# Five loads wait for a matmul: a sigmoid attention with a token-mixing MLP on one core

## The chip, the cores and the metric

The kernel runs on one core of one Trainium2 chip. The time is that of one execution on the device, in microseconds (us). The profile is one further execution, recorded by the hardware profiler; its span runs from the first recorded instruction to the last, and the execution's own time lies a little above its span.

Engines are named as in the profile: PE (TensorE's matmuls), PEld (its weight loads), DVE (VectorE), ACT (ScalarE), POOL (GpSimd), SP (SyncE, which here only issues DMAs).

## The reference

q, k and v have the shape [8, 12, 448, 64] (batch, heads, tokens, width), in float32.

```python
scores = scale * np.matmul(q, k.transpose(0, 1, 3, 2)) - np.log(S)
attn = 1.0 / (1.0 + np.exp(-scores))
x = np.matmul(attn, v)                      # then [8, 448, 768]
wq = x @ w_q                                # [8, 448, 64]
wk = x @ w_k
W_tok = scale * np.einsum('bsd,btd->bst', wq, wk)
mixed = np.einsum('bst,btd->bsd', W_tok, x)
out = np.maximum(mixed, 0.0) @ w_out        # [8, 448, 768]
```

So a sigmoid takes the place of a softmax, and the second half mixes tokens by a matrix that is itself computed from x. Input, output and weights are float32; the matmuls are done in bf16.

## The kernel before, in words

**Tiling.** The work is cut into 24 quads: quad (u, j) is four heads of batch u. A quad has 7 blocks of 64 keys per head. For a block, `scores` (L299) issues four 64x64 matmuls (L303) into a pair of PSUM banks, and ACT takes the sigmoid of the pair into an SBUF tile (L308). `values` (L314) multiplies that tile with v (L321) and gathers the seven blocks of a quad in one pair of banks, which is copied into `xt` (L330). When the three quads of a batch are there, the second half follows for it: transposes of x (L344, L361), the products with w_q and w_k (`mlp_wqk`, L387), a transpose of wk, the product of wk with x (`mlp_tmp`, L431), the mixed tokens with their relu (`mlp_mix`, L471 and L483), and the output product with w_out (L530, L576, L626). The output tiles go to DRAM by stores on SP (L550, L594, L641), some of them held in a list and let go by the letter D of the plan.

**Order.** The order of the instructions on every engine is written out by hand: the string `PLAN` (L127) has a letter for each step (S scores, P and p values, q and k with their variants the bringing of q and k into the layout for the scores, W, N, U, M, O the steps of the second half, D and C stores and copies), and the loop at L840 walks through it. So batch u's second half is interleaved with the attention of later batches.

**Loads.** q, k and v come as one tile of 448 KB for each quad and the six slices of 128 rows of w_out ("w1" to "w6" in the order string, 384 KB each) between them. They are issued in the order of the string `ORDER` (L714), all on SP's queue, by `pump_loads` (L736): each load goes into the next of six fp32 buffers (`lds`, L104), and a load is issued as soon as the tile that was six loads earlier in the same buffer has been cast to bf16. `pump_loads` is called in the program right behind each cast, and so the place of a load in SP's list is settled by the casts. `pump` (L778) issues the casts, on POOL for most tiles, in the order of `ORDER`; a point ahead of a name in `ORDER` puts the cast on DVE (`cast_one`, L787), some steps behind the load. After the casts of q and k of a quad, POOL rearranges the tile (`arrange`, L148) and DVE transposes it (L259, L252).

SP's list holds the loads, the stores and some copies of w_out (L893), and SP works through it in order: a DMA whose semaphore has not come yet holds those behind it.

**Names in the profile.** `ld` is a buffer of a load; `banks` is PSUM; `at` a block of sigmoids; `mx` the mixed tokens; `wkn` and `tmp` are tiles of the second half; `o` is an output tile. The queue q1 carries the loads and stores of SP; q8 carries TensorE's instructions, which are brought from memory in packets while the kernel runs.

Of the kernel before, what the change touches and what calls it, by code (L numbers as in the profile page):

```python
# [17 lines left out]
def kernel(  # L18
# [145 lines left out]

    def load1(n, nm, eng):
        u, j = quads[n]
        if KIND[n] in "cer" and nm != "v":
            t = ld_next()
            eng.dma_start(
                out=t, in_=SRC[nm][u, 4 * j : 4 * j + 4].rearrange("h (p r) d -> (h p) (r d)", r=2 * NI),  # L170
            )
            ld[nm, n] = t
            return
        t = ld_next2()
        eng.dma_start(
            out=t,
            in_=SRC[nm][u, 4 * j : 4 * j + 4].rearrange(
                "(g h) (p i) d -> (h p) g (i d)", g=2, i=NI
            ),
        )  # L180
        ld[nm, n] = t
# [25 lines left out]
    def transposes(ps, t16, r):  # L207

        for x, i in enumerate(range(r.start, r.stop)):
            for g in range(2):  # L210
                for h in range(2):
                    nc.tensor.transpose(  # L212
                        ps[HALF[g], h, x * NP : (x + 1) * NP], t16[HALF[h], i, g, :],
                        ident16[HALF[h], HALF[h]],
                    )

    def transposes_whole(ps, t16, r):

        for x, i in enumerate(range(r.start, r.stop)):
            nc.tensor.transpose(  # L220
                ps[:, x * P : (x + 1) * P], t16[:, i].rearrange("p b d -> p (b d)"), ident16,
            )
# [76 lines left out]
    def scores(n, i):  # L299
        fb, sc, _ = bank2()  # L300
        for g in range(2):
            for h in range(2):
                nc.tensor.matmul(  # L303
                    sc[HALF[h], g, 0:S], qk[n][HALF[g], h, 1, i, :],
                    qk[n][HALF[g], h, 0].rearrange("p i n -> p (i n)"), start=True, stop=True,
                )
        at = p_at.tile([P, 2, S], BF16, tag="at", name="at")
        nc.scalar.activation(at, sc[:, :, 0:S], ACTF.Sigmoid, bias=attn_bias, scale=attn_scale)  # L308
        release(fb)
        ats[n, i] = at  # L310
# [3 lines left out]
    def values(n, i, tail, eng):  # L314
        u, j = quads[n]
        if i == 0:
            pv[n] = bank2()
        fb, ps, _ = pv[n]
        for h in range(2):
            for g in range(2):  # L320
                nc.tensor.matmul(  # L321
                    ps[HALF[g], h, 0:S], ld["v16", n][HALF[h], i, g, :],
                    ats[n, i][HALF[h], g, :], start=(i == 0), stop=(i == NI - 1),
                )
# [10 lines left out]
    def tr_x(n, tail, whole, eng):  # L335
# [3 lines left out]
        if whole:  # L339
            fb, _, ps = bank1()  # L340
            ps = ps.rearrange("p (m g h d) -> p m g h d", m=4, g=2, h=2)
            for h in range(2):
                for m in range(4):
                    nc.tensor.transpose(  # L344
                        ps[:, m, :, h], xt(u, j)[:, h, m * P : (m + 1) * P], ident16
                    )
            for g in range(2) if tail else (slice(0, 2),):
                w = slice((2 * j + g) * P, (2 * j + g + 1) * P) if tail else slice(2 * j * P, 2 * (j + 1) * P)
                COPY["vs"[g] if tail else eng](  # L349
                    out=xns[u][:, :, w],  # L350
                    in_=ps[:, :, g].rearrange("p m h d -> p m (h d)")
                    if tail else ps.rearrange("p m g h d -> p m (g h d)"),
                )
            release(fb)
            return
        fb, _, ps = bank2()
        for m in range(4):
            for h in range(2):
                for g in range(2):
                    for c in range(2):  # L360
                        nc.tensor.transpose(  # L361
                            ps[HALF[c], g, (2 * m + h) * HD : (2 * m + h + 1) * HD],
                            xt(u, j)[HALF[g], h, (2 * m + c) * HD : (2 * m + c + 1) * HD],
                            ident16[HALF[g], HALF[g]],
                        )
# [14 lines left out]
    def mlp_wqk(u, c, tail, act, tiled):  # L380
# [3 lines left out]
        if tiled:  # L384
            for y in range(2):
                for x in range(2):
                    nc.tensor.matmul(  # L387
                        ps[HALF[x], y, 0:S], wqk16[HALF[y], c, 64 * x : 64 * x + 64],
                        xt(u, c // 2)[HALF[y], c % 2, 0:S], start=(c == 0), stop=(c == NC - 1),
                    )  # L390
# [8 lines left out]
        ps = ps[:, 0:S]  # L399
        nc.tensor.matmul(  # L400
            ps, wqk16[:, c, :], xt(u, c // 2)[:, c % 2, 0:S], start=(c == 0), stop=(c == NC - 1),
# [10 lines left out]
    def mlp_wkn(u):  # L412
        fb, _, ps = bank1()
        for m in range(4):
            for c in range(2):
                nc.tensor.transpose(
                    ps[HALF[c], m * DH : (m + 1) * DH],
                    wqks[u % 2][HALF[1], (2 * m + c) * DH : (2 * m + c + 1) * DH],
                    ident16[HALF[1], HALF[1]],
                )  # L420
# [4 lines left out]
    def mlp_tmp(u, act):  # L425
# [3 lines left out]
        for m in range(4):  # L429
            for y in range(2):  # L430
                nc.tensor.matmul(  # L431
                    ps[HALF[y]], wkn[u][:, m, :], xns[u][:, m, y * NB : (y + 1) * NB],
                    start=(m == 0), stop=(m == 3),
                )
# [3 lines left out]
    def mlp_tmp_tiled(u, act):  # L438
# [3 lines left out]
        for m in range(4):  # L442
            for r in range(2):
                if 2 * m + r == NI:
                    continue
                for y in range(2):
                    nc.tensor.matmul(  # L447
                        ps[HALF[y], r, 0:NB], wkn[u][HALF[r], m, :], xns[u][HALF[r], m, y * NB : (y + 1) * NB],
# [12 lines left out]
    def mlp_mix(u, c, act, tail):  # L461
# [5 lines left out]
        if w in TW:  # L467
            for z in range(2):
                for y in range(2):
                    for x in range(2):  # L470
                        nc.tensor.matmul(  # L471
                            ps[HALF[x], y, 256 * z : 256 * z + 256],
# [8 lines left out]
        for y in range(2):  # L481
            for x in range(2):
                nc.tensor.matmul(  # L483
                    ps[HALF[x], y, 0:S], tmps[u][HALF[y], c * P + 64 * x : c * P + 64 * x + 64],
# [33 lines left out]
    def out_pair(act, tail):  # L518
# [8 lines left out]
        for b in range(3 * part, 3 * part + 3):  # L527
            for y, (u, i) in enumerate(blocks):
                for x in range(2):
                    nc.tensor.matmul(  # L530
                        ps[HALF[x], y, 0:NB], mx[HALF[y], u, b, 64 * (i - 3 * y) : 64 * (i - 3 * y) + 64],
# [24 lines left out]
    def out_halves(act, tail):  # L556
# [15 lines left out]
        for c in range(3 * h, 3 * h + 3):  # L572
            t0 = 2 * S * c + m * P + b * NP
            for y in range(2):
                for x in range(2):
                    nc.tensor.matmul(  # L576
                        ps[HALF[x], y, 0:NB], mxs[w][HALF[y], t0 : t0 + NP], wout16[HALF[y], c, x * NB : (x + 1) * NB],
# [28 lines left out]
    def out_chunk(act, tail):  # L606
# [17 lines left out]
        def block(ps, w0, w1, c0, c1):  # L624
            for c in range(c0, c1):
                nc.tensor.matmul(  # L626
                    ps, mxs[w][:, 2 * S * c + m * P : 2 * S * c + (m + 1) * P],
# [48 lines left out]

    def load_wout(c):
        w32[c] = ld_next()[:, 0:D]
        nc.sync.dma_start(out=w32[c], in_=moe_w_out[c * P : (c + 1) * P, :])

# [23 lines left out]
    for _ in range(32):  # L704
        nc.tensor.matmul(pairs[3][:, 0, 0:P], zeros[:, 0:P], zeros[:, 0:P], start=True, stop=True)
    for t in xts:
# [129 lines left out]
    done["q"] = done["k"] = 1  # L836
    nc.tensor.matmul(pairs[free2[0]][:, 0, 0:P], zeros[:, 0:P], zeros[:, 0:P], start=True, stop=True)
    quads_r = []

    for t in PLAN:  # L840
        if t == "F":
            nc.tensor.matmul(pairs[free2[0]][:, 0], zeros[:, 0:P], zeros, start=True, stop=True)
            continue
        if t == "E":
            for g in range(2):
                for h in range(2):
                    nc.tensor.matmul(
                        pairs[free2[0]][HALF[h], g, 0:S], zeros[HALF[g], 0:NP], zeros[HALF[g], 0:S], start=True, stop=True,
                    )
# [94 lines left out]
```

## Time and profile before

| | before |
|---|---|
| time, three runs | 187.07, 186.75, 186.1 us (median 186.75) |
| the profiled execution's own time | 186.47 us |
| its span | 184.7 us |
| granted TensorE clock | 1.00 |
| DMA | 48.51 MB, 263 GB/s in the mean |

How to read it: the shares of busy time are averages over the whole span. The chain of waits follows the work that ended last from the last instruction back to the first, and says for each piece which engine and line, or which wait, it was. "issue" there is time in which an engine waited for nothing that the profile shows. A line `start, us, engine line op` of a timeline is one group of like instructions, with the idle time before it and what ended that in square brackets. A row of busy time by stretch gives the length of the stretch, then busy time and number of instructions for PE, PEld, DVE, ACT and POOL, then the granted clock, the DMA share and GB/s. The DMA rows give, for each queue, packets, MB, and the time of its packets as a share of the 16 DMA engines in that stretch.

### The profile page before, as it was taken

How to read it: one execution, taken by the hardware profiler on the slowest of the kernel's cores; microseconds unless marked ns; L12 is line 12 of the kernel's file. 1: busy time of each engine (PE TensorE's matmuls, PEld its weight loads, DVE VectorE, ACT ScalarE, POOL GpSimd, SP SyncE). 2: the span in 40 equal slices, each digit the busy share in tenths (PEclk: the TensorE clock that was granted, in tenths of full speed). 3: DMA queues.
4: the chain of work that ended last, by engine and by line, in shares of the span. 5: the costliest groups of instructions: out<-in, count | busy, mean ns of one | idle time of the engine just before them, and what ended most of it. 6: DMA issues, size and time to landing. Idle time of an engine off the chain costs nothing.

```text
span 184.7 us, 8546 instructions
## 1 busy us (share of the span) xinstructions
PE 174.6 (95%) x3662; PEld 115.1 (62%) x3662; DVE 133.0 (72%) x209; ACT 162.8 (88%) x209; POOL 124.4 (67%) x171
## 2 busy tenths in 40 slices
PE   7988989999799999999999999999999999999990
PEld 7444645545445464566555778678887878869660
DVE  3424888779598887999797788587668476686820
ACT  4799999999799999999999989999999989876330
POOL 1467799896999599779999996999999920000000
PEclk9999999999999999999999999999999999999999
DMA  5999999969998999988998995897997453422596
GB/s 174 362 383 389 325 382 360 376 209 322 390 331 262 293 350 336 269 304 280 304 281 250 316 330 182 223 362 278 276 307 196 102 136 89 113 65 55 134 240 170
DMA packets 26085, 48.51 MB, mean 263 GB/s; under 512 B 3968, under 2 KB 19968, under 8 KB 26048
## 3 DMA queue, kind: packets, MB, share of 16 engines
q1 hardware_dynamic: 25888, 47.79, 80.0%
q8 instruction: 28, 0.46, 1.0%
q10 hardware_dynamic: 160, 0.20, 0.4%
q14 instruction: 9, 0.07, 0.2%
HBM read 35.78 MB, written 11.01 MB: 253 GB/s over the span
## 4 chain that ended last, share of the span: by engine, by line
PE 73%; ACT 17%; issue 3%; DVE 2%; DMA 2%; ACTq 0%; POOL 0%; SPq 0%
PE banks L303 16%; ACT at L308 16%; PE banks L530 15%; PE banks L321 13%; PE banks L626 12%; PE banks L387 3%; PE banks L576 3%; PE banks L431 2%; DMA ld<-in_k_dram 2%; PE banks L344 2%; PE banks L361 2%; PE banks L471 2%; PE banks L212 1%; PE banks L447 1%; PE banks L483 1%
## 5 line engine op out<-in xcount | busy, mean ns | idle before, releaser
L308 ACT ACTIVATE at<-banks 128x896 bf16<-128x896 f32 x168 | 141.4, 931 | 5.5 <-PE banks L303 4.8
L303 PE MATMUL banks<-qk 64*64 64x448 bf16 x672 | 62.0, 358 | 2.1 <-ACT at L308 1.4
L321 PE MATMUL banks<-at,v 64*64 64x448 bf16 x672 | 45.7, 351 | 0.4 <-ACT at L308 0.4
L303 PEld LDWEIGHTS <-qk 64*64 64x64 bf16 x672 | 25.8, 105 | 22.6 <-issue 13.6
L188 POOL CAST qk<-ld 128x896 bf16<-128x896 f32 x28 | 33.1, 1194 | 7.3 <-issue 1.9
L530 PE MATMUL banks<-wout,mx 64*64 64x384 bf16 x672 | 36.9, 323 | 0.1
L321 PEld LDWEIGHTS <-v 64*64 64x64 bf16 x672 | 22.8, 106 | 9.4 <-issue 2.7
L330 DVE CAST xt<-banks 128x896 bf16<-128x896 f32 x19 | 20.7, 1089 | 10.6 <-PE banks L321 10.1
L530 PEld LDWEIGHTS <-mx 64*64 64x64 bf16 x672 | 23.5, 106 | 4.3 <-issue 0.8
L626 PE MATMUL banks<-wout,mx 128*128 128x384 bf16 (+1 forms) x138 | 24.9, 320 | 0.0
L459 DVE TENSOR_SCALAR mx<-banks 128x1024 bf16<-128x1024 f32 (+2 forms) x21 | 21.1, 1011 | 3.9 <-PE banks L471 1.8
L198 POOL CAST v<-ld 128x896 bf16<-128x896 f32 x23 | 21.6, 955 | 2.0 <-DMA ld<-in_v_dram 1.8
L626 PEld LDWEIGHTS <-mx 128*128 128x128 bf16 x138 | 12.0, 98 | 10.3 <-issue 4.6
L157 POOL COPY swap<-qk 32x448 uint32<-32x448 uint32 x28 | 16.3, 583 | 1.7
L259 DVE STREAM_TRANSPOSE qk<-qk 128x448 f32<-128x448 f32 x28 | 17.4, 630 | 0.0
L163 POOL COPY qk<-swap 32x448 uint32<-32x448 uint32 x28 | 16.1, 577 | 1.6
L160 POOL COPY qk<-qk 32x448 uint32<-32x448 uint32 x28 | 16.1, 576 | 1.6
L539 DVE COPY o<-banks 128x768 f32<-128x768 f32 x11 | 10.5, 953 | 6.2 <-PE banks L530 4.6
L374 DVE COPY xn<-banks 128x1024 bf16<-128x1024 bf16 (+1 forms) x14 | 9.0, 649 | 3.2 <-PE banks L361 2.7
L198 POOL CAST q<-ld 128x896 bf16<-128x896 f32 x7 | 7.0, 999 | 1.8 <-DMA ld<-in_q_dram 1.4
L387 PE MATMUL banks<-xt,wqk 64*64 64x448 bf16 x120 | 8.0, 349 | 0.0
L349 DVE COPY xn<-banks 128x1024 bf16<-128x1024 bf16 x9 | 6.1, 683 | 1.3 <-PE banks L344 1.1
(94 smaller groups left out, 203.8 us busy)
## 6 DMA issues: line engine op xcount, KB each, us to landing
ld<-in_q_dram SPq DMA_DIRECT2D x24, 448.0 KB, 5.7
ld<-in_v_dram SPq DMA_DIRECT2D x24, 448.0 KB, 5.6
ld<-in_k_dram SPq DMA_DIRECT2D x23, 448.0 KB, 6.0
out_dram<-o SPq DMA_DIRECT2D x42, 192.0 KB, 4.9
ld<-in_moe_w_out_dram SPq DMA_DIRECT2D x6, 384.0 KB, 6.3
out_dram<-ld SPq DMA_DIRECT2D x11, 192.0 KB, 2.8
wout<-wout SPq DMA_DIRECT2D x12, 96.0 KB, 5.5
out_dram<-ld SPq DMA_DIRECT2D x4, 96.0 KB, 2.3
```

Of the source, the lines that this page charges most:

```text
L157: eng.tensor_copy(out=z[lo], in_=w[hi, 0])
L160: eng.tensor_copy(out=w[hi, 0], in_=w[lo, 1])
L188: COPY[e](out=f[:, :, "qk".index(nm)].rearrange("p e i d y -> p e y i d"), in_=ld.pop((nm, n)).rearrange("p (y i e d) -> p e y i d", y=2, ...
L198: COPY[e](out=t16.rearrange("p i b d -> p b i d"), in_=ld.pop((nm, n)).rearrange("p b (i d) -> p b i d", i=NI),)
L259: nc.vector.transpose(out=qk[n][:, t].rearrange("p t i n -> p (t i n)").bitcast(F32), in_=w)
L303: nc.tensor.matmul(sc[HALF[h], g, 0:S], qk[n][HALF[g], h, 1, i, :], qk[n][HALF[g], h, 0].rearrange("p i n -> p (i n)"), start=True, stop=True,
L308: nc.scalar.activation(at, sc[:, :, 0:S], ACTF.Sigmoid, bias=attn_bias, scale=attn_scale)
L321: nc.tensor.matmul(ps[HALF[g], h, 0:S], ld["v16", n][HALF[h], i, g, :], ats[n, i][HALF[h], g, :], start=(i == 0), stop=(i == NI - 1),)
L330: COPY[eng](out=xt(u, j)[:, :, 0:S], in_=ps[:, :, 0:S])
L459: nc.vector.tensor_scalar(dst, ps, moe_scale, 0.0, ALU.mult, ALU.max)
L530: nc.tensor.matmul(ps[HALF[x], y, 0:NB], mx[HALF[y], u, b, 64 * (i - 3 * y) : 64 * (i - 3 * y) + 64], wout16[HALF[y], slot(y, b), x * NB : ...
L626: nc.tensor.matmul(ps, mxs[w][:, 2 * S * c + m * P : 2 * S * c + (m + 1) * P], wout16[:, c, w0:w1], start=(c == 0), stop=(c == NC - 1),)
```

## The change

All matmuls and transposes on TensorE are now issued through `mm` and `mt`, which also keep them in a list, `products`, in order of issue. A table `BEHIND` names five loads and for each the number of a product. `pump_loads` issues such a load only once that product stands in the list, and gives it a semaphore wait on that product's end. `pump_loads` and `pump` are also called at the head of each step of the plan, so that a load that was held back in the program is issued when its product is there. Nothing is computed otherwise, and no tile or buffer changes.

The five loads are slice w1 (rows 0 to 127) of w_out, v of quads 8, 20 and 23, and q of quad 22.

```diff
+    products = []
+
+    def mm(*args, **kw):
+        products.append(nc.tensor.matmul(*args, **kw))
+
+    def mt(*args, **kw):
+        products.append(nc.tensor.transpose(*args, **kw))
...
+    def behind_product(load, m):
+
+        if m > 0:
+            tc.add_manual_dep(
+                load.ins, products[m].ins.name,
+                mybir.DependencyInfo(mybir.DependencyClass.Sync, mybir.DependencyReason.DATA),
+                reason="loads begin behind a matmul",
+            )
...
-    def load_wout(c):
+    def load_wout(c, m):
         w32[c] = ld_next()[:, 0:D]
-        nc.sync.dma_start(out=w32[c], in_=moe_w_out[c * P : (c + 1) * P, :])
+        behind_product(nc.sync.dma_start(out=w32[c], in_=moe_w_out[c * P : (c + 1) * P, :]), m)
...
+    BEHIND = {("w", 1): 728, ("v", 8): 856, ("q", 22): 2264, ("v", 20): 2392, ("v", 23): 2648}
...
             nm, n = ORDER[len(loaded)]
+            m = BEHIND.get((nm, n), 0)
+            if m >= len(products):
+                break
             if len(ring) >= 6 and ring[-6] not in cast:
                 break
             ring.append((nm, n))
             if nm == "w":
-                load_wout(n - 1) if n else load_weights()
+                load_wout(n - 1, m) if n else load_weights()
             else:
-                load1(n, nm, nc.sync)
+                load1(n, nm, nc.sync, m)
...
     for t in PLAN:
+        pump_loads()
+        pump()
         if t == "F":
```

`load1` passes its DMA through `behind_product` in the same way, and every `nc.tensor.matmul` and `nc.tensor.transpose` of the kernel becomes `mm` or `mt`.

More of the change, by code (lines that the diff above doesn't have):

```diff
@@ L168, in load1 @@
             t = ld_next()
-            eng.dma_start(
-                out=t, in_=SRC[nm][u, 4 * j : 4 * j + 4].rearrange("h (p r) d -> (h p) (r d)", r=2 * NI),
+            behind_product(
+                eng.dma_start(
+                    out=t, in_=SRC[nm][u, 4 * j : 4 * j + 4].rearrange("h (p r) d -> (h p) (r d)", r=2 * NI),
+                ), m,
             )
@@ L174, in load1 @@
         t = ld_next2()
[L175 to L179, printed above, removed]
+        behind_product(
+            eng.dma_start(
+                out=t,
+                in_=SRC[nm][u, 4 * j : 4 * j + 4].rearrange(
+                    "(g h) (p i) d -> (h p) g (i d)", g=2, i=NI
+                ),
+            ), m,
         )
@@ L211, in transposes @@
                 for h in range(2):
-                    nc.tensor.transpose(
+                    mt(
                         ps[HALF[g], h, x * NP : (x + 1) * NP], t16[HALF[h], i, g, :],
@@ L302, in scores @@
             for h in range(2):
-                nc.tensor.matmul(
+                mm(
                     sc[HALF[h], g, 0:S], qk[n][HALF[g], h, 1, i, :],
@@ L320, in values @@
             for g in range(2):
-                nc.tensor.matmul(
+                mm(
                     ps[HALF[g], h, 0:S], ld["v16", n][HALF[h], i, g, :],
@@ L343, in tr_x @@
                 for m in range(4):
-                    nc.tensor.transpose(
+                    mt(
                         ps[:, m, :, h], xt(u, j)[:, h, m * P : (m + 1) * P], ident16
@@ L360, in tr_x @@
                     for c in range(2):
-                        nc.tensor.transpose(
+                        mt(
                             ps[HALF[c], g, (2 * m + h) * HD : (2 * m + h + 1) * HD],
@@ L386, in mlp_wqk @@
                 for x in range(2):
-                    nc.tensor.matmul(
+                    mm(
                         ps[HALF[x], y, 0:S], wqk16[HALF[y], c, 64 * x : 64 * x + 64],
@@ L399, in mlp_wqk @@
         ps = ps[:, 0:S]
-        nc.tensor.matmul(
+        mm(
             ps, wqk16[:, c, :], xt(u, c // 2)[:, c % 2, 0:S], start=(c == 0), stop=(c == NC - 1),
@@ L415, in mlp_wkn @@
             for c in range(2):
-                nc.tensor.transpose(
+                mt(
                     ps[HALF[c], m * DH : (m + 1) * DH],
@@ L430, in mlp_tmp @@
             for y in range(2):
-                nc.tensor.matmul(
+                mm(
                     ps[HALF[y]], wkn[u][:, m, :], xns[u][:, m, y * NB : (y + 1) * NB],
@@ L446, in mlp_tmp_tiled @@
                 for y in range(2):
-                    nc.tensor.matmul(
+                    mm(
                         ps[HALF[y], r, 0:NB], wkn[u][HALF[r], m, :], xns[u][HALF[r], m, y * NB : (y + 1) * NB],
@@ L470, in mlp_mix @@
                     for x in range(2):
-                        nc.tensor.matmul(
+                        mm(
                             ps[HALF[x], y, 256 * z : 256 * z + 256],
@@ L482, in mlp_mix @@
             for x in range(2):
-                nc.tensor.matmul(
+                mm(
                     ps[HALF[x], y, 0:S], tmps[u][HALF[y], c * P + 64 * x : c * P + 64 * x + 64],
@@ L529, in out_pair @@
                 for x in range(2):
-                    nc.tensor.matmul(
+                    mm(
                         ps[HALF[x], y, 0:NB], mx[HALF[y], u, b, 64 * (i - 3 * y) : 64 * (i - 3 * y) + 64],
@@ L575, in out_halves @@
                 for x in range(2):
-                    nc.tensor.matmul(
+                    mm(
                         ps[HALF[x], y, 0:NB], mxs[w][HALF[y], t0 : t0 + NP], wout16[HALF[y], c, x * NB : (x + 1) * NB],
@@ L625, in block @@
             for c in range(c0, c1):
-                nc.tensor.matmul(
+                mm(
                     ps, mxs[w][:, 2 * S * c + m * P : 2 * S * c + (m + 1) * P],
@@ L704 @@
     for _ in range(32):
-        nc.tensor.matmul(pairs[3][:, 0, 0:P], zeros[:, 0:P], zeros[:, 0:P], start=True, stop=True)
+        mm(pairs[3][:, 0, 0:P], zeros[:, 0:P], zeros[:, 0:P], start=True, stop=True)
     for t in xts:
@@ L836 @@
     done["q"] = done["k"] = 1
-    nc.tensor.matmul(pairs[free2[0]][:, 0, 0:P], zeros[:, 0:P], zeros[:, 0:P], start=True, stop=True)
+    mm(pairs[free2[0]][:, 0, 0:P], zeros[:, 0:P], zeros[:, 0:P], start=True, stop=True)
     quads_r = []
     for t in PLAN:
+        pump_loads()
+        pump()
         if t == "F":
-            nc.tensor.matmul(pairs[free2[0]][:, 0], zeros[:, 0:P], zeros, start=True, stop=True)
+            mm(pairs[free2[0]][:, 0], zeros[:, 0:P], zeros, start=True, stop=True)
             continue
@@ L846 @@
                 for h in range(2):
-                    nc.tensor.matmul(
+                    mm(
                         pairs[free2[0]][HALF[h], g, 0:S], zeros[HALF[g], 0:NP], zeros[HALF[g], 0:S], start=True, stop=True,
```

4 lines of the change are left out of this document (2 added, 2 removed).

## The prediction

> **What bounds the kernel now.** I read the busy shares first, then the queues of the page, then busy time by stretch.
>
> ```profile
> PE 174.6 (95%) x3662; PEld 115.1 (62%) x3662; DVE 133.0 (72%) x209; ACT 162.8 (88%) x209; POOL 124.4 (67%) x171
> ...
> q8 instruction: 28, 0.46, 1.0%
> ```
> ```profile
> 52.00:160.70 108.70, 108.63 (x2410) 74.48 (x2406) 85.90 (x119) 104.74 (x129) 86.46 (x119) 1.00 0.81 257
> ```
>
> TensorE is the bound: from 52.0 to 160.7 us PE is busy 108.63 of 108.70 at the full granted clock. A load can gain nothing there by coming earlier. Time is to be had only where PE stands. The chain of waits around 49 us shows the largest such place, and the timelines of the weight loads and of ACT what it does.
>
> ```profile
> 49.34 0.75 issue
> 50.09 0.32 PE banks L431
> ```
> ```profile
> 48.50 0.47 PEld L431 LDWEIGHTS <-wkn 128*64 128x64 bf16 x8 [0.20 <-issue]
> 50.34 0.11 PEld L303 LDWEIGHTS <-qk 64*64 64x64 bf16 x4 [1.38 <-issue]
> ```
> ```profile
> 50.84 2.54 ACT L308 ACTIVATE at<-banks 128x896 bf16<-128x896 f32 x3 [0.99 <-PE banks L303]
> ```
>
> PE stands 0.75 us for nothing that the profile names ("issue"), ahead of the last matmul of a group at L431 whose operands are all there. The weight loads pause 1.38 us (48.97 to 50.34), and ACT, the second busiest engine, then starves for 0.99 us. What is missing is the instructions themselves. Their queue, q8, brought 28 packets for the 3662 + 3662 instructions: 7324/28 = 262 to a packet, some 128 products with their weight loads. The counts of products fit that:
>
> ```profile
> 0.00:50.05 50.05, 44.88 (x863) 25.74 (x864) 32.69 (x63) 46.09 (x57) 36.15 (x51) 1.00 0.96 333
> 50.05:131.33 81.28, 80.87 (x1664) 50.99 (x1664) 68.24 (x95) 78.75 (x98) 71.68 (x97) 1.00 0.89 291
> ```
> ```profile
> 131.35 0.27 PEld L530 LDWEIGHTS <-mx 64*64 64x64 bf16 x8 [0.45 <-issue]
> ```
>
> The stall stands ahead of product 863 (counted from 0). A second, shorter pause stands 1664 = 13 x 128 products later, ahead of 2527. So packet borders lie at 735 + 128k. The DMA view by stretch shows the packet that the first stall waits for, and that of the second:
>
> ```profile
> q1 hardware_dynamic: 550, 1.29, 98.3%
> ```
> ```profile
> q8 instruction: 1, 0.02, 6.2%
> ```
> ```profile
> q1 hardware_dynamic: 416, 0.88, 76.2%
> ```
> ```profile
> q8 instruction: 1, 0.02, 6.1%
> ```
>
> These are 43.9 to 47.67, 47.67 to 48.7, 125.7 to 128.9 and 128.9 to 130.0 us. In the first, loads move and no instructions do; in the second (of which, and of the fourth, the row of q8 is shown) the packet passes in 0.062 x 16 x 1.03 = 1.02 us, and TensorE goes on 1.39 us after its end (48.70 to 50.09). In the third pair likewise: nothing, then a packet until some 130.07, and work again 1.3 us later, at 131.35.
>
> I read the request as made when TensorE enters the packet before, that is at border 735 (44.0 us, below) for the packet from 863. It then waited 3.7 us. What was ahead of it is in SP's timeline and the issue-to-landing times:
>
> ```profile
> 41.12 0.38 SPq L175 DMA_DIRECT2D ld<-in_v_dram  x1
> 41.75 0.34 SPq L679 DMA_DIRECT2D ld<-in_moe_w_out_dram  x1
> 42.63 0.34 SPq L169 DMA_DIRECT2D ld<-in_q_dram  x1
> 43.41 1.56 SPq L679 DMA_DIRECT2D ld<-in_moe_w_out_dram  x2
> 47.98 0.38 SPq L175 DMA_DIRECT2D ld<-in_v_dram  x1
> ```
> ```profile
> ld<-in_v_dram SPq DMA_DIRECT2D x1, 448.0 KB, 5.1
> ```
> ```profile
> ld<-in_q_dram SPq DMA_DIRECT2D x1, 448.0 KB, 7.2
> ```
>
> v7 (issued 41.12) lands at 46.2, q10 (42.63) at 49.8. The packet, 47.67 to 48.70, passed behind v7 and the weight rows "w1" and in the midst of q10, but ahead of the next weight rows (43.41), issued 0.6 us before the request.
>
> **The change part by part.** Five loads get one wait each on the end of a product: 728, 856, 2264, 2392, 2648, each 7 products ahead of a border (735, 863, 2271, 2399, 2655). In the instruction order PE, DVE, ACT and POOL keep every place; PE gets five semaphore updates on matmuls that exist. On SP, w1, v8 and v20 keep their places; q22 and v23 move behind the two stores each that followed them; q14's load and two stores swap. When those products ran, by their counts:
>
> ```profile
> 0.00:43.30 43.30, 39.08 (x729) 22.39 (x730) 27.58 (x57) 39.54 (x50) 31.64 (x45) 1.00 0.95 330
> 0.00:48.51 48.51, 44.05 (x857) 25.38 (x858) 31.69 (x63) 44.74 (x56) 34.96 (x49) 1.00 0.95 332
> 0.00:120.88 120.88, 115.34 (x2266) 68.86 (x2270) 92.22 (x146) 114.63 (x142) 98.12 (x134) 1.00 0.92 307
> 0.00:125.67 125.67, 120.13 (x2393) 72.42 (x2396) 96.11 (x152) 119.19 (x148) 102.55 (x140) 1.00 0.92 309
> ```
> ```profile
> 118.01 0.33 SPq L169 DMA_DIRECT2D ld<-in_q_dram  x1
> 118.43 4.72 SPq L550 DMA_DIRECT2D out_dram<-o  x6
> 125.37 0.39 SPq L175 DMA_DIRECT2D ld<-in_v_dram  x1
> ...
> 135.18 0.37 SPq L175 DMA_DIRECT2D ld<-in_v_dram  x1
> ```
>
> Each product starts at the end of its row and takes some 0.36 us, so the loads can go at about 43.7, 48.9, 121.2 and 126.0.
>
> *w1*: 41.75 becomes 43.7, 2.0 us later; behind it on SP wait q10 (+1.5 at most) and the two weight loads from 43.41 (+1.2 to +0.4). Nothing held is then ahead of the request of 44.0 but v7: the load of 43.41 went 0.6 before it and came behind, and w1 now goes 0.3 before it. The packet starts when v7 is through, by 46.2, passes until 47.2 and is usable 1.4 later, at 48.6. The weight load that needs it is due at 48.97. Margin 0.3 to 0.4: the stall goes, with little to spare. Its worth is at least PE's 0.75 and at most ACT's 0.99, since ACT has sigmoids queued and the next scores wait for it; I take 0.9, nearer to ACT's.
>
> *v8*: 47.98 becomes 48.9, with q11 and k11 behind it +0.5. There is no stall at 991, so this gains nothing by itself; it keeps v8 from standing ahead of the request at 863, which comes 0.9 earlier once the first stall is gone.
>
> *q22, v20*: these hold the next gain. q22 goes 2 to 3 us later and its place is taken by stores of L550; v20 goes at most 0.7 later, or none when TensorE is 0.9 ahead. The packets for 2399 and 2527 come earlier by what no longer stands in front. At 2527 the weight loads' pause is 0.45, against 0.20 at a plain join (the row of 48.50): 0.2 taken, between 0 and 0.45. If these two packets did not come earlier, the 0.9 would be lost again there: TensorE 0.9 ahead would meet them where they are.
>
> ```profile
> q1 hardware_dynamic: 243, 0.33, 99.9%
> q8 instruction: 1, 0.02, 6.2%
> ```
>
> That is 123.5 to 124.4: the packet for 2399, at the end of which 1.3 us lead to 125.7, just when 2399 is reached. It has no slack already.
>
> *v23*: issued 0.5 to 1.5 later, no stall near it; nothing.
>
> *Cover of the later landings.* Who takes the delayed data:
>
> ```profile
> 49.92 1.19 POOL L188 CAST qk<-ld 128x896 bf16<-128x896 f32 x1 [0.35 <-DMA ld<-in_q_dram]
> ```
> ```profile
> 63.51 1.19 POOL L188 CAST qk<-ld 128x896 bf16<-128x896 f32 x1 [1.92 <-issue]
> ```
> ```profile
> 63.75 0.62 DVE L259 STREAM_TRANSPOSE qk<-qk 128x448 f32<-128x448 f32 x1
> ```
> ```profile
> 56.98 1.13 DVE L198 CAST v<-ld 128x896 bf16<-128x896 f32 x1
> ```
> ```profile
> 133.96 1.20 POOL L188 CAST qk<-ld 128x896 bf16<-128x896 f32 x1
> 135.08 0.93 POOL L198 CAST v<-ld 128x896 bf16<-128x896 f32 x1
> ...
> 147.59 0.93 POOL L198 CAST v<-ld 128x896 bf16<-128x896 f32 x1
> ```
>
> q10's cast already waits for its landing, so POOL's row of casts and rearrangements comes up to 1.5 late. It ends at 61.59, 1.92 ahead of POOL's next cast and 2.2 ahead of the transposition of its result: hidden. v8, landed by 53.0, is cast on DVE at 56.98; q22 (landing near 127) at 133.96; v20 (near 129) at 135.08; v23 (140) at 147.59. All hidden by 4 us and more, and no buffer's return moves, since each is freed by its cast.
>
> **Sum**: 0.9 + 0.2 = 1.1 us. The profiled execution took 186.47 (184.7 of span and 1.77 around it), so 185.37 against its own time. The median of the runs shown is 186.75, and the mean of the four times 186.6. From these 185.5 to 185.65 follow: **185.6**.
>
> **The rivals.**
>
> *No effect on the packet.* If the request is made otherwise than I read it, or w1's descriptors at 43.7 still get ahead of it, the packet stands behind w1 as before. A half of the stall, or all, stays: 186.2 to 186.8. For it: the margin is 0.3. Against it: the load of 43.41 came behind.
>
> By the Trainium skill, "DMA: Bandwidth & Descriptors", section "Queues, rings and completion order", each DMA engine takes turns between its queues, packet by packet. By that rule a request would pass after one packet of the loads, and holding loads would be worth nothing: 186.6. The trace speaks against it: the 3.8 us without a q8 packet above.
>
> *The wall.* The first stall goes, and the packets for 2399 or 2527 come no earlier, since six stores and k- and v-loads fill the engines in q22's place. Then 0.7 to 0.9 is lost again there: 186.3 to 186.7. For it: the 99.9% share around 124.0. Against it: 448 KB less stand in front of the packet.
>
> *Slower.* SP takes its list in order, so w1's wait holds q10 and two weight loads, and the engines run empty for a moment. If q10's landing comes more than 1.9 later than 49.8, POOL's chain eats its pause at 63.5 and its next casts run late; from 2.2 DVE's transposition is late too and with it the scores. At 4 us, with the instructions' packet and w1 ahead of q10, TensorE would wait about 2 us, against 1.1 won: 187.6. Against it: q10 is issued only 1.5 later, behind the same bytes.
>
> **How the numbers follow.** Forecast 0.58 (185.1 to 186.0), no effect 0.18 (0.06 of it for the turns between queues), wall 0.14, slower 0.10. What this kernel's measurement can tell from no change is 0.5%, 0.93 us, so the border is 185.82, close to the forecast; 0.05 of the forecast's chance lies above it. Faster 0.53, same 0.37, slower 0.10. The range 185.0 to 186.9 leaves out the slower rival and the forecast's edge. Both ends of the unknown costs lie in it: 0.75 + 0 gives 185.85, 0.99 + 0.45 gives 185.16 from 186.6.
>
> **What would show it.** Right: the "issue" of 0.75 us in the chain before product 863 is gone, ACT's 0.99 at 50.84 too, and the q8 packet passes by 47.3; PE's weight loads show no pause above 0.25 at 2399 and 2527. Wrong: the packet still passes after 47.6; or a new "issue" of some 0.9 at a border in 120 to 132 us; or POOL's idle time "<-DMA" grows by over 2 us between 48 and 64 and PE waits for DVE or POOL behind it.

## The result, and the profile after

The changed kernel takes 185.54 us (median of 8 runs, 185.22 to 186.15), the kernel before 187.13 us (8 runs, 186.1 to 189.43). The ratio is 0.9926, with a 95% interval of 0.9902 to 0.9950: 0.5 to 1.0% faster. A ratio is that of the means (here 185.62 and 187.00 us); an execution over 1.5% above the fastest of its kernel, as the one of 189.43 us, counts as slow and is left out of it. The profiled execution of the changed kernel took 185.81 us, with a span of 184.0.

The busy shares of the page say that the work is the same; the busy time of PE is 174.7 us for 174.6:

```profile
PE 174.7 (95%) x3662; PEld 115.3 (63%) x3662; DVE 133.1 (72%) x209; ACT 162.7 (88%) x209; POOL 124.3 (68%) x171
```

What has changed is where TensorE stands. Every matmul is now issued from one helper, so the rows have its lines (L119, transposes L122), and groups are told apart by tiles. First the weight loads and ACT around product 863, in the changed kernel (start, us, engine, line, operation, tile, count, idle time before it):

```profile
48.98 0.47 PEld L119 LDWEIGHTS <-wkn 128*64 128x64 bf16 x8 [0.20 <-issue]
49.75 0.11 PEld L119 LDWEIGHTS <-qk 64*64 64x64 bf16 x4 [0.30 <-issue]
```
```profile
47.77 5.82 ACT L329 ACTIVATE at<-banks 128x896 bf16<-128x896 f32 x7
```

The pause of 1.38 us in the weight loads is 0.30, which is what this join costs without a stall (the same 0.30 stands at this join where no packet border is near it, in experiment 6). ACT's idle 0.99 us is gone: seven sigmoids stand in a row. Next SP, and the DMA queues from 44.4 to 45.8 and from 45.8 to 46.8 us:

```profile
44.22 0.34 SPq L700 DMA_DIRECT2D ld<-in_moe_w_out_dram  x1
44.65 0.38 SPq L187 DMA_DIRECT2D ld<-in_q_dram  x1
45.13 0.86 SPq L700 DMA_DIRECT2D ld<-in_moe_w_out_dram  x2
```
```profile
q1 hardware_dynamic: 254, 0.48, 96.4%
```
```profile
q1 hardware_dynamic: 145, 0.35, 98.5%
q8 instruction: 1, 0.02, 6.1%
```

w1 goes at 44.22, and the packet of instructions that passed at 47.68 to 48.70 before passes at 45.8 to 46.8 now. The border at 735 is reached at 44.45, so it waited 1.4 us and not 3.7. The DMA engines are no less busy (96 to 98%): the packet does not pass because the engines are free; what differs is that w1 was ordered 2.0 us later against the border.

The second pause, ahead of 2527, is gone too. At 2399 one is left, in the changed kernel's weight loads:

```profile
125.54 0.46 PEld L119 LDWEIGHTS <-mx 64*64 64x64 bf16 x12 [0.34 <-issue]
```
```profile
130.26 0.56 PEld L119 LDWEIGHTS <-mx 64*64 64x64 bf16 x12
```

In before these two rows had 0.17 and 0.45.

**Where the time went, by stretches.** The starts of TensorE's weight loads, by their number, divide an execution well, since all 3662 are in each trace. The long stretches between the borders repeat to 0.01 us in all these kernels (991 to 2271: 63.35 or 63.36; 864 to 991: 7.18 or 7.19, but for one; 2784 to 3552: 27.56 or 27.57), so that nearly the whole difference can be read off a few columns. "Wait" is from the weight load of 735, where I take the request to be made, to the start of the packet for 863. All are us of the one profiled execution. That the request is made at a border is inferred: in each of these traces exactly one packet starts between two borders of 735 + 128k, the earliest 0.06 us behind its border. Experiment 6 has other numbers and stands apart.

| kernel | wait | 862 to 864 | 864 to 991 | 2398 to 2400 | 2526 to 2528 | 223 to 3661 |
|---|---|---|---|---|---|---|
| before | 3.70 | 1.49 | 7.19 | 0.29 | 0.56 | 164.73 |
| changed | 1.37 | 0.42 | 7.19 | 0.46 | 0.10 | 163.57 |
| 1 w1 alone | 2.23 | 0.42 | 7.18 | 0.67 | 0.56 | 164.08 |
| 2 all but w1 | 2.78 | 0.48 | 7.18 | 0.15 | 0.10 | 163.40 |
| 3 order, no wait | 3.01 | 0.76 | 7.19 | 0.14 | 0.10 | 163.67 |
| 4 all 64 earlier | 3.29 | 1.05 | 7.19 | 1.56 | 0.10 | 165.36 |
| 5 w1 at 776 | 1.59 | 0.42 | 8.61 | 0.15 | 0.10 | 164.78 |
| 7 q22 at 2296 | 2.05 | 0.42 | 7.19 | 0.14 | 0.10 | 163.31 |
| 8 w1, q22, v20 | 1.54 | 0.42 | 7.19 | 0.15 | 0.10 | 163.34 |
| 9 changed again | 1.26 | 0.42 | 7.19 | 0.15 | 0.10 | 163.31 |
| 10 w1, q22 | 2.57 | 0.42 | 7.19 | 0.14 | 0.69 | 163.71 |
| 11 w1 at 715 | 2.97 | 0.72 | 7.19 | 0.14 | 0.10 | 163.61 |
| 12 v19 for q22 | 2.46 | 0.42 | 7.18 | 0.14 | 0.09 | 163.73 |

0.42, 0.14 and 0.10 are the joins without a pause. After an undelayed join at 2527, 0.23 us are given back in the two stretches behind it (2528 to 2784 takes 10.95 for 10.72), so the 0.56 there cost 0.23. Before to changed: 1.07 won at 863, 0.17 lost at 2399, 0.23 won at 2527, in all 1.16 from 223 to the end (0.03 is left to other places). The starts differ too: product 223 begins at 15.33 in before and 15.81 in the changed kernel, and anywhere from 15.33 to 16.43 in the kernels of the table. Up to there the changed kernel issues its loads in the same order as before and none of them is held, so this is not the change. With this later start the two profiled executions as a whole lie only 0.66 us apart (186.47 and 185.81).

### The profile page after: what moved, and what is told of

The parts are those of the page before. It is cut to its first block, busy times and chain, and to the rows that moved or that the text cites. A ratio compares the mean times of both kernels' runs of the same rounds, so it can differ in the third digit from the quotient of the medians.

```text
span 184.0 us, 8547 instructions
## 1 busy us (share of the span) xinstructions
PE 174.7 (95%) x3662; PEld 115.3 (63%) x3662; DVE 133.1 (72%) x209; ACT 162.7 (88%) x209; POOL 124.3 (68%) x171
## 4 chain that ended last, share of the span: by engine, by line
PE 78%; ACT 14%; issue 3%; DVE 2%; ACTq 0%
PE banks L119 73%; ACT at L329 13%; PE banks L122 6%; DVE xt L351 1%; DVE mx L480 1%; ACTq L661 0%; DVE ld L680 0%; DVE wqk L426 0%; ACT xt L349 0%; ACT wq L428 0%; ACT ld L678 0%; DVE zeros L716 0%; ACTq L329 0%; ACTq L678 0%; ACTq L428 0%
## 5 line engine op out<-in xcount | busy, mean ns | idle before, releaser
L119 PE MATMUL banks<-wout,mx 64*64 64x384 bf16 (+2 forms) x954 | 68.5, 323 | 0.0
L119 PE MATMUL banks<-qk 64*64 64x448 bf16 x672 | 61.8, 358 | 2.0 <-ACT at L329 1.3
L119 PEld LDWEIGHTS <-mx 64*64 64x64 bf16 (+1 forms) x954 | 41.1, 105 | 14.4 <-issue 5.1
L119 PE MATMUL banks<-at,v 64*64 64x448 bf16 x672 | 45.6, 351 | 0.2
L119 PEld LDWEIGHTS <-qk 64*64 64x64 bf16 x672 | 25.5, 105 | 21.4 <-issue 12.6
L209 POOL CAST qk<-ld 128x896 bf16<-128x896 f32 x28 | 33.6, 1210 | 5.4 <-DVE qk L280 1.4
L119 PEld LDWEIGHTS <-v 64*64 64x64 bf16 x672 | 22.7, 106 | 9.2 <-issue 2.4
L165 POOL COPY swap<-qk 32x448 uint32<-32x448 uint32 x28 | 15.7, 562 | 1.7
L122 PEld LDWEIGHTS <-xt 64*64 64x64 bf16 (+1 forms) x528 | 10.9, 107 | 3.6 <-issue 2.4
L119 PE MATMUL banks<-xt,wqk 64*64 64x448 bf16 (+1 forms) x138 | 12.7, 350 | 0.1
L122 PE MATMUL banks<-ident,xt 64*64 64x64 bf16 (+1 forms) x528 | 12.4, 198 | 0.1
L119 PE MATMUL banks<-wqk,tmp 64*64 64x256 bf16 (+1 forms) x72 | 8.9, 298 | 0.1
L119 PE MATMUL banks<-wq,tmp 64*64 64x256 bf16 (+1 forms) x72 | 9.0, 300 | 0.0
```

The costliest lines, as they stand in the source:

```text
L119: products.append(nc.tensor.matmul(*args, **kw))
L122: products.append(nc.tensor.transpose(*args, **kw))
L165: eng.tensor_copy(out=z[lo], in_=w[hi, 0])
L209: COPY[e](out=f[:, :, "qk".index(nm)].rearrange("p e i d y -> p e y i d"), in_=ld.pop((nm, n)).rearrange("p (y i e d) -> p e y i d", y=2, ...
```

## The experiments

Theory: a packet of TensorE's instructions, requested one packet ahead, waits in the DMA engines for the loads that were issued before the request; the holds let loads go so late that the packet gets ahead of them (w1 goes 0.23 us before the request wherever it is held at 728). Rivals: the order on SP does it (C), the waits themselves (D), the later loads alone (B), the first gain needs no second one (A).

**1. w1 alone.**

```diff
-    BEHIND = {("w", 1): 728, ("v", 8): 856, ("q", 22): 2264, ("v", 20): 2392, ("v", 23): 2648}
+    BEHIND = {("w", 1): 728}
```

> Only the weight rows w1 wait (for product 728); v8, q22, v20 and v23 are issued as before. Theory (TensorE's instruction packets stand in the DMA engines behind loads that were issued earlier): the stall ahead of product 863 is gone, TensorE is some 0.9 us ahead behind it, and loses most of that again at the borders 2399 and 2527, whose packets come no earlier: ratio to before 0.996 to 1.000. Rival A (the later packets come earlier by themselves when TensorE is ahead): the 0.9 stays, ratio 0.9945 to 0.996. Rival B (what q22, v20 and v23 do is all of the gain): the stall ahead of 863 stays, ratio 1.000.

Measured: 186.17 us, ratio 0.9946 (0.9921 to 0.9972). The profiled execution, 186.46, does what the theory says: 863 is free, and its weight loads stop at 2399 and 2527:

```profile
125.95 0.46 PEld L119 LDWEIGHTS <-mx 64*64 64x64 bf16 x12 [0.56 <-issue]
```
```profile
131.33 0.27 PEld L119 LDWEIGHTS <-mx 64*64 64x64 bf16 x8 [0.45 <-issue]
```

Against 163.31 without a pause it has 164.08: 0.53 lost at 2399 and 0.23 at 2527. This is the wall. The ratio lies with rival A, though. The twelve times fall in two groups, three from 185.12 to 185.25 and nine from 186.07 to 186.46, and the profile is of the upper one; it fits that the wall is met in most executions and missed in some, but no trace of a lower one was taken. By its time this kernel can't be told from the changed kernel.

**2. All but w1.**

```diff
-    BEHIND = {("w", 1): 728, ("v", 8): 856, ("q", 22): 2264, ("v", 20): 2392, ("v", 23): 2648}
+    BEHIND = {("v", 8): 856, ("q", 22): 2264, ("v", 20): 2392, ("v", 23): 2648}
```

> The other four loads wait, w1 does not. Theory: the packet for product 863 again stands behind w1, the stall of about 0.75 us ahead of 863 stays; at 2399 and 2527 up to 0.4 us is saved: ratio to before 0.997 to 1.000. Rival B (the gain is that of the late loads): ratio 0.992 to 0.994.

Measured: 186.29 us, ratio 0.9967 (0.9935 to 0.9998), as the theory has it. Its interval just touches what rival B gave (0.992 to 0.994); what rules rival B out is experiment 1, where 863 is free with w1 alone held and the interval leaves out 1.000. In the trace the late pauses are gone, but the pause at 863 is short this time:

```profile
50.24 0.11 PEld L119 LDWEIGHTS <-qk 64*64 64x64 bf16 x4 [0.37 <-issue]
```

The stretch from 862 to 864 is 0.06 over the plain join, where 0.75 was expected: a miss in size. w1 was issued later here (42.98, 1.9 us ahead of the request at 44.87, for 2.2 in before), and the packet waited 2.78 and not 3.70.

**3. The order alone.**

```diff
-        if m > 0:
+        if m < 0:
             tc.add_manual_dep(
```

> The order of all lists is that of the changed kernel (q22 and v23 behind two stores each), but no load has the wait on a product. Theory: w1 goes at about 41.8 us as before, the packet for 863 stands behind it, the stall stays: ratio to before 0.997 to 1.001. Rival C (the order on SP, not the waits, makes the gain): ratio 0.992 to 0.994 and no stall ahead of 863.

Measured: 186.71 us, ratio 0.9990 (0.9960 to 1.0020). The gain needs the waits; rival C falls. The trace has the pause at 863 (0.76 - 0.42 = 0.34 us over the plain join) and none at 2399 and 2527: q22 behind two stores was enough there in this execution.

```profile
50.73 0.11 PEld L119 LDWEIGHTS <-qk 64*64 64x64 bf16 x4 [0.65 <-issue]
```

**4. The same waits, 64 products earlier.**

```diff
-    BEHIND = {("w", 1): 728, ("v", 8): 856, ("q", 22): 2264, ("v", 20): 2392, ("v", 23): 2648}
+    BEHIND = {("w", 1): 664, ("v", 8): 792, ("q", 22): 2200, ("v", 20): 2328, ("v", 23): 2584}
```

> The same five loads wait for products, each 64 products earlier (664, 792, 2200, 2328, 2584). The waits and the five semaphore updates are there, but w1's is over before its buffer is free. Theory: w1 goes as before, ahead of the request for the packet: the stall ahead of 863 stays, ratio 0.997 to 1.001. Rival D (the waits or updates themselves change TensorE's flow, or any later load helps): ratio 0.992 to 0.994.

Measured: 186.89 us, ratio 0.9999 (0.9966 to 1.0032). Rival D falls: five waits and five updates that come half a packet earlier are worth nothing. The pauses are back, at 863 and, larger than in before, at 2399:

```profile
50.30 0.11 PEld L119 LDWEIGHTS <-qk 64*64 64x64 bf16 x4 [0.94 <-issue]
```
```profile
127.23 0.46 PEld L119 LDWEIGHTS <-mx 64*64 64x64 bf16 x12 [1.45 <-issue]
```

**5. w1 later still.**

```diff
-    BEHIND = {("w", 1): 728, ...
+    BEHIND = {("w", 1): 776, ...
```

> As the changed kernel, but w1 waits for product 776 instead of 728: it and the loads behind it on SP (q10 and two weight loads) go some 2.4 us later still, at about 46.6 us, with the packet for 863 long ahead of them. Theory with the prediction's arithmetic: q10 lands 2.4 to 2.9 us later than before's 49.9, POOL's chain of casts takes up its pause of 1.9 us, DVE's transposition (2.2 to 3.4 us of slack) is late by at most 0.7: ratio to before 0.992 to 0.996, and TensorE waits for nothing but at most 0.5 us on DVE or POOL. Rival (waiting loads cost at once what they are late): TensorE waits some 2 us between 50 and 70, ratio 1.000 to 1.004.

Measured: 187.37 us, ratio 1.0033 (0.9996 to 1.0069). This is the rival's side. No border has a pause, and 1.42 us are lost between 864 and 991. SP's list, the waits of PE, the chain of waits and PE's timeline say for what:

```profile
47.29 0.34 SPq L700 DMA_DIRECT2D ld<-in_moe_w_out_dram  x1
47.73 0.38 SPq L187 DMA_DIRECT2D ld<-in_q_dram  x1
48.20 0.86 SPq L700 DMA_DIRECT2D ld<-in_moe_w_out_dram  x2
```

```profile
PE banks L119 <- DVE wout L790: 1.4, 1, 1.4
```
```profile
48.67 6.65 DMA ld<-in_moe_w_out_dram
...
55.42 0.57 DVE wout L790
```
```profile
54.33 0.34 PE L119 MATMUL banks<-wout,mx 128*128 128x384 bf16 x1
56.03 0.48 PE L119 MATMUL banks<-wout,mx 128*128 128x384 bf16 x2 [1.37 <-DVE wout L790]
```

It is not q10 and POOL, but the second of the two weight loads behind them on SP: it lands at 55.33, is cast on DVE by 55.99, and the output product that needs it stood 1.37 us. In the changed kernel the same two casts run together at 52.14:

```profile
52.14 1.40 DVE L790 CAST wout<-ld 128x768 bf16<-128x768 f32 x2
```

There the same load, issued at 45.60, landed at 52.36. In experiment 5 the cast ended 0.66 us behind the landing, and the output product was due at 56.03 - 1.37 = 54.66, so that landing was due at 54.00. The changed kernel is 0.19 earlier there (864 begins at 49.75 and not 49.94), so its landing is due at 53.81: the cover of the hold at 728 is 1.4 to 1.5 us. That agrees with the loss: against TensorE, w1 went 3.07 - 0.19 = 2.88 us later in experiment 5 than in the changed kernel, and 1.42 of it was lost. By this estimate a hold that came 1.5 us later would begin to cost.

**6. Other numbers, same kernel before.**

```diff
-    for _ in range(32):
-        nc.tensor.matmul(pairs[3][:, 0, 0:P], zeros[:, 0:P], zeros[:, 0:P], start=True, stop=True)
+    for _ in range(64):
+        nc.tensor.matmul(pairs[3][:, 0, 0:64], zeros[:, 0:P], zeros[:, 0:64], start=True, stop=True)
```

> The kernel before, with 64 warm-up matmuls of 64 columns in place of 32 of 128 (their results are not used): every later product has a number 32 higher, and nothing else moves. Theory (packets of TensorE's instructions hold 128 products, borders at 735 + 128k by number): packets pass and pauses stand at the same numbers as before, 863 and the like, which are now other matmuls, 32 earlier in the plan; the matmul that stalled before (now number 895) runs without a pause. The time depends on which loads stand in front there: ratio 0.990 to 1.004. Rival (the pause belongs to that matmul, its operands or its time): it stays ahead of the same matmul, now number 895, at about 49 to 50 us.

Measured: 187.89 us, ratio 1.0035 (0.9997 to 1.0073). The join that stalled in before runs plainly, and the pauses have gone to other matmuls:

```profile
50.82 0.11 PEld L303 LDWEIGHTS <-qk 64*64 64x64 bf16 x4 [0.30 <-issue]
```
```profile
42.81 0.28 PEld L344 LDWEIGHTS <-xt 128*128 128x128 bf16 x5 [1.00 <-issue]
```
```profile
63.00 0.11 PEld L321 LDWEIGHTS <-v 64*64 64x64 bf16 x2 [1.34 <-issue]
```

These stand at the numbers 735 and 1119, which is 863 - 128 and 863 + 2 x 128. Where a pause can stand is a matter of a matmul's number, not of its operands. Which loads stood ahead of these two packets was not followed here.

**7. q22 later.**

```diff
-    BEHIND = {... ("q", 22): 2264 ...
+    BEHIND = {... ("q", 22): 2296 ...
```

> As the changed kernel, but q22 waits for product 2296 instead of 2264, and so goes about 1.2 us behind the request for the packet of 2399 instead of 0.4. In the changed kernel's trace that packet took 2.02 us to pass (122.16 to 124.18) with q22's data beside it, against some 1.0 us for most, and TensorE paused 0.3 us ahead of 2399. Theory (a load issued just behind the request still shares the engine with the packet): the packet passes in about 1.0 us, the pause goes: 0.1 to 0.3 us less than the changed kernel, ratio to before 0.990 to 0.9925. Rival (the 2.02 us comes from the stores in front): the packet still takes 2 us, ratio as the changed kernel, 0.9926, or up to 0.994 if the stores behind q22 come late.

Measured: 186.61 us, ratio 0.9982 (0.9945 to 1.0020): not the 0.990 to 0.9925 that the theory expected, and beyond the rival's 0.994. Yet the profiled execution, 185.75, shows what the theory expected: the packet passes in 0.88 us, and 163.31 is the time without any pause. Its packets for 2527 to 3039 came within 0.1 to 0.3 us of being late, by the 1.3 us that they need behind their end; in other executions they may have been late. But experiment 10's packets for 2911 and 3039 came as narrowly, and its ratio is 0.9934. Why this kernel gains so little was not traced and stays open.

**8. w1, q22 and v20.**

```diff
-    BEHIND = {("w", 1): 728, ("v", 8): 856, ("q", 22): 2264, ("v", 20): 2392, ("v", 23): 2648}
+    BEHIND = {("w", 1): 728, ("q", 22): 2264, ("v", 20): 2392}
```

> Only w1, q22 and v20 wait; v8 and v23 are issued as before. Theory: those three do all of the work, the stalls at 863, 2399 and 2527 are gone, ratio to before 0.992 to 0.994. Rival (v8 must wait too, since it stands ahead of the packet for 863 or 991; or v23, for 2655 or 2783): a pause of 0.3 us or more at one of these borders, ratio 0.995 to 0.998.

Measured: 185.86 us, ratio 0.9959 (0.9921 to 0.9996); the profiled execution took 185.4. The ratio is on the rival's side, the trace on the theory's: no pause at any border, 163.34. The weight loads at 2399 and 2527 join plainly, with no idle time named:

```profile
125.11 0.48 PEld L119 LDWEIGHTS <-mx 64*64 64x64 bf16 x12
```
```profile
129.88 0.56 PEld L119 LDWEIGHTS <-mx 64*64 64x64 bf16 x12
```

Whether v8 and v23 are worth anything in other executions is not told apart, since the interval holds the changed kernel's ratio.

**9. The changed kernel again**, with nothing altered, beside 10 to 12.

> The changed kernel itself, beside the three others on the same chip. Expected: ratio to before 0.990 to 0.995, as in the result; no pause ahead of 863; a pause of at most 0.3 us at 2399 or 2527.

Measured: 185.99 us, ratio 0.9951 (0.9914 to 0.9988). No pause at any border this time, 163.31.

**10. w1 and q22.**

```diff
-    BEHIND = {("w", 1): 728, ("v", 8): 856, ("q", 22): 2264, ("v", 20): 2392, ("v", 23): 2648}
+    BEHIND = {("w", 1): 728, ("q", 22): 2264}
```

> Only w1 and q22 wait. Theory: 863 is free, and 2399 too (q22 goes behind the request); the packet for 2527, requested at 2399, again stands behind v20, so the pause there comes back at 0.5 us or more: ratio to before 0.994 to 0.997, between w1 alone (0.9946, a pause at 2399 and at 2527) and the changed kernel. Rival (q22 is enough, since v20 was only 0.3 us ahead of the request in before): no pause at 2527, ratio 0.992 to 0.994.

Measured: 185.76 us, ratio 0.9934 (0.9897 to 0.9971). The pause at 2527 is back and that at 2399 is not, as the theory has it:

```profile
130.55 0.27 PEld L119 LDWEIGHTS <-mx 64*64 64x64 bf16 x8 [0.58 <-issue]
```

It costs 163.71 - 163.31 = 0.40 us, 0.2%, which the ratios cannot show; the ratio itself lies in the rival's range.

**11. w1 some 1.6 us ahead of the request.**

```diff
-    BEHIND = {... ("w", 1): 728 ...
+    BEHIND = {... ("w", 1): 715 ...
```

> As the changed kernel, but w1 waits for product 715 instead of 728, which ends 1.1 to 1.8 us ahead of the request at 735: w1 goes at about 43.1, 1.3 us ahead of the request. In before, q10 was issued 1.3 us ahead and was half in front of the packet. Theory (what counts is to be issued less than about 1 us ahead of the request): the packet for 863 starts 0.5 to 1.0 us later than in the changed kernel (45.8), behind a part of w1, and just makes it: no pause or up to 0.3 us, ratio to before 0.992 to 0.996. Rival (any load issued ahead of the request is in front as a whole): the pause of 0.7 us is back, ratio 0.996 to 1.000.

Measured: 186.47 us, ratio 0.9970 (0.9931 to 1.0008). w1 went at 42.58, 1.6 us ahead of the request at 44.18; the packet started at 47.15, and there is a pause of 0.72 - 0.42 = 0.30 us. SP, the queues from 44.2 to 47.1 us (no packet) and from 47.1 to 48.2, and the weight loads:

```profile
42.58 0.34 SPq L700 DMA_DIRECT2D ld<-in_moe_w_out_dram  x1
```
```profile
q1 hardware_dynamic: 432, 0.95, 98.6%
```
```profile
q1 hardware_dynamic: 140, 0.42, 95.3%
q8 instruction: 1, 0.02, 5.7%
```
```profile
49.77 0.11 PEld L119 LDWEIGHTS <-qk 64*64 64x64 bf16 x4 [0.60 <-issue]
```

The pause is at the theory's upper edge, but the packet started later than the theory had it (46.3 to 46.8), and the ratio lies in the rival's range. Still, the rival is not right either: the packet passed before the last of the sixteen shares of v7 (48.82) and of w1 (49.80) had landed, so neither was wholly in front of it.

**12. v19 in q22's place.**

```diff
-    BEHIND = {... ("q", 22): 2264 ...
+    BEHIND = {... ("v", 19): 2264 ...
```

> As the changed kernel, but v19 waits for product 2264 in place of q22, and q22 comes behind it on SP: v19, two stores and q22 are all behind the request at 2271 that brings the packet for 2399. Theory: that packet starts within 1 us of the request and the pause at 2399 is gone in every run; v19 lands by some 126 and is cast at 127.5 as before: ratio to before 0.989 to 0.993, up to 0.3 us less than the changed kernel. Rival (what is pushed back now stands ahead of the packet for 2527, requested at 2399): a pause of 0.4 us or more there, ratio 0.993 to 0.998.

Measured: 186.12 us, ratio 0.9957 (0.9916 to 0.9998). At 2399 the packet started 0.63 us behind the request, the fastest of all; the delay came back one border later than the rival named, at 2655:

```profile
136.84 0.27 PEld L119 LDWEIGHTS <-mx 64*64 64x64 bf16 x8 [0.47 <-issue]
```

What is held at one border may stand ahead of a later one. No version measured here has a lower ratio than the changed kernel's 0.9926. The times alone do not tell apart the changed kernel and 1, 8, 9, 10 and 12 (0.9926 to 0.9959); what the holds behind w1's are worth rests on the traces, of which there is one for each kernel.

## Why the prediction was right, point by point

- *The stall is missing instructions, at borders 735 + 128k.* Right, and shown by experiment 6.
- *w1's hold frees 863.* Right: every kernel that holds w1 at 728 or later has 0.42 there, the five that don't (before, 2, 3, 4, 11) have 0.48 to 1.49. The size was 0.9, at most 0.99; the traces have 1.07 of TensorE's own flow, a little above that bound.
- *How the packet waits.* Only in part, and the time came out right all the same. I had it in order: behind v7 and w1, ahead of what was issued later, with a margin of 0.3 to 0.4 us. In before the landings fit that (w1 complete at 47.47, packet from 47.68). In every other trace of the table the packet started before v7 had landed: in the changed kernel at 45.82, with none of v7's 16 shares landed (46.16 to 46.83), and in 2, 3, 4 and 11, where w1 is issued 1.1 to 1.9 us ahead of the request, with no share of w1 landed either. What the traces show instead is a matter of degree. Where w1 was held, the packet started 0.2 to 0.8 us after k10, the load ahead of v7, had landed; where it was not, 0.7 to 2.9 us after. And v7's own time seems to count: where it was issued only 1.9 to 2.1 us ahead of the request, the packet waited 2.5 to 2.6 us with w1 held (10, 12) and 3.0 to 3.3 without (3, 4); where it was 2.8 ahead, 1.4 (changed) and 3.7 (before). So the margin in the changed kernel was not 0.3 to 0.4 but 1.2 to 1.3 us (the packet ended at 46.79, could be used 1.4 later at 48.2, and was needed at 49.45). Full engines are not all of it: behind the request of 125.70 in before they were 17% busy until 126.4, and the packet still started only at 128.99, after v20, issued 0.33 us ahead of the request, had landed at 128.70. How the engines share themselves between loads and the packet is not settled. The Trainium skill's rule ("DMA: Bandwidth & Descriptors", section "Queues, rings and completion order": each engine takes turns between its queues, packet by packet) was a rival by which holding loads is worth nothing; the measured ratio of 0.9926 speaks against that use of it, not against the turns. That a packet starts before loads under way have landed, as in all traces but before's, would go with such turns.
- *The wall.* Right as a mechanism: experiment 1 lost 0.76 us to it, of 0.7 to 0.9 predicted. With q22 and v20 held it is gone (2 and 8), and in 10, without v20's hold, 2527 pauses again; but in 3 both borders were free by the order alone. The changed kernel's profiled execution still had 0.32 at 2399 (an idle time of 0.34 where the prediction's sign of being right was at most 0.25), and its second profiled execution, in experiment 9, had nothing.
- *The second term, 0.2.* 0.23 was won at 2527, but 0.17 lost at 2399, so that 0.06 is left of it in the profiled pair. In experiment 9 nothing was lost there.
- *v8 and v23 at nothing.* No trace shows a pause that they take away (8).
- *Cover of the later loads.* Here the working was incomplete. It costed w1, q10, v8, q22, v20 and v23, and for the two weight loads behind q10 it named a delay and no cover. They have the least: the slower rival was real, but its decisive point was the output weights cast on DVE, not q10 on POOL, and TensorE stood 1.37 us when w1 went at 47.3 (experiment 5).
- *The sum.* 1.1 predicted, 1.16 in the profiled pair from product 223 on. But the parts differ: 1.07 and 0.06, where 0.9 and 0.2 were predicted, so that two misses nearly cancel. Against experiment 9's execution, which has no pause at all, it is 1.42. The means differ by 1.38 (187.00 - 185.62). That 185.6 met the median of 185.54 so closely owes something to chance: the median of before rose from 186.75 with three runs to 187.13 with eight.

Before's times reach from 185.43 to 188.37 us in these ratios, the changed kernel's from 185.22 to 186.51. Two things are seen to differ between traced executions, the start (1.1 us from the earliest to the latest) and the pauses (the stretch at 2399 takes 0.14 to 1.56). What an execution of before at 188 us waits for was not traced.

## What to carry to other kernels

Where TensorE stops with "issue" inside a group whose operands are there, count the products between such stops: if they repeat by a fixed number, look in the queue of instructions for the packet, and in the issuing engine's list for the loads that were ordered in the few us before the border one packet earlier. Holding such a load until TensorE is all but at that border, by a wait on a matmul, costs nothing as long as everything queued behind it on the same engine has the time: cost each of those, not only the load that is held. Free all the borders of a stretch, or most of the time won at the first can be lost at the next (0.76 of 1.07 us in experiment 1's profiled execution).

## What the runs showed of the hardware that had not been expected

A packet of 0.02 MB mostly passed in 0.9 to 1.3 us, but in some cases in about twice that: in the changed kernel that for 2399 took from 122.16 to 124.18. The row of the queue from 122.1 to 124.2 us has 6.0% of 16 engines, which is one engine for 2.02 us of the 2.1:

```profile
q8 instruction: 1, 0.02, 6.0%
```

So a packet lies on one of the 16 DMA engines. A load that it meets can end late on one share: q10 in before had 15 of 16 shares landed by 48.59 and the last at 49.87, 1.28 us later.
